# Block-sparse attention and a routed expert layer on one core: keys and values stacked on 128 partitions, first chunks in sequence order, two key sets and six V tiles

## The chip, the cores and the metric

The kernel runs on one core of one Trainium2 chip. TensorE (PE) multiplies 128x128 tiles from SBUF into PSUM; its weight loads are shown as an engine of their own (PEld). VectorE (DVE), ScalarE (ACT) and GpSimd (POOL) do the element-wise work, and SyncE (SP) issues most transfers. Each engine has its own in-order queue; semaphores link them. The metric is the device time of one execution in microseconds; lower is better.

## The reference

Two blocks run one after the other, all in float32. The first is attention with a block mask: 4 sequences, 8 heads, 768 positions, 64 dimensions a head, blocks of 32 positions (24 blocks). A query block sees its own block and its two neighbours, the first and the last block, and three blocks drawn at random for it; the first and the last query block see all blocks.

```python
mask = np.abs(blk_i - blk_j) <= window
mask = mask | (blk_i == 0) | (blk_j == 0) | (blk_i == n_blocks - 1) | (blk_j == n_blocks - 1)
for qb in range(n_blocks):
    for kb in sampled_blocks[qb]:
        mask[qb*block:(qb+1)*block, kb*block:(kb+1)*block] = True
attn = softmax(where(mask, q @ k.T / sqrt(D), -1e9));  out = attn @ v
```

The second takes the 3072 rows of 512 that result. Each row goes to one of 8 experts, the one whose embedding has the largest cosine with the row, and comes back as `gate * (relu(x @ w1[e]) @ w2[e])`, where w1 is 512x1024 and w2 is 1024x512 per expert.

## The kernel before

Attention runs in 24 steps over chunks of 128 query rows. Sequences go in pairs (0 and 1, then 2 and 3): `place(n)` maps chunk n to a pair, a chunk position c (0 to 5) and a member i of the pair, and chunks alternate between the members. Rows are shifted by 32, so that chunk c = 0 holds the last and the first block (the "end" rows, which see all keys) and two ordinary blocks; every other chunk has two halves of 64 rows. A pair of adjacent chunks shares one transfer of Q (`load_q`), one V tile (`load_v`, `vt`) and one gather of the random blocks' V (`gather_v`, `vg_ring`, two buffers).

For one chunk the work on PE is this.

- `turn_q` transposes Q into `qt`, which is block-diagonal over the two heads of a head pair: rows 0 to 63 are nonzero for head 0 only, rows 64 to 127 for head 1 only.
- `score_near` scores the queries against their own 64-key window and against the 64 end keys (`ke`, the last and the first block). It uses quarters of the array (64 rows x 64 columns), one head at a time; `near_at` says where each result goes.
- `score_far` scores the queries, per block of 32, against a gathered set of 128 keys: three random blocks and the outer neighbour block. Both heads go in one product.
- `weigh_near` and `weigh_far` multiply the exponentials with V into `av`. `vg0` is a copy of the end blocks' V (`keep_ends`), and `near_v` copies the neighbour block's V into `vg`.
- For c = 0, `score_ends` and `weigh_ends` do the end rows against all 768 keys.
- `normalize` divides by the sum of the weights; `turn_x` and `chunk_logits` (one step later) make the router's logits; `route` does the rest of the routing and ends with the transfer of the rows to `x_dram`.

`turn_x` and `turn_q` share one PSUM buffer, `xg_ps`. Scores and K transposes share a ring of two PSUM buffers, `big`.

Keys are transposed per head pair by `turn_k` from `kraw` (loaded by `load_k`; g counts 4 sequences x 4 head pairs). There are three key sets `kt` (sequence 3 uses that of sequence 0 again), and seven V tiles. `gather_k` copies the key blocks that a chunk needs into `kg`: one random block on DVE, two on POOL, the neighbours on DVE.

The order of the work in attention is written out by hand, in `attention_fast` (L1242): per step s, scores of chunk s, weighing of chunk s - 1, logits of chunk s - 2, with K transposes (`turning`), K loads (`loading`), V loads, Q loads and gathers placed by step number. SP issues in that order and waits at the first transfer whose buffer is not free. `after_step` (L1223) places the routing, the early dispatch and the loads of the first expert tile's weights at given steps. Before step 0, the kernel loads Q of both sequences, K of both, and all of the first pair's V.

After attention, 5 expert tiles of rows from the first pair and 20 tiles of the rest follow, each with 4 MB of weights in a ring of three (`fetch_weights`, L1091). The pool `wp` opens at step 18, in memory that the attention's short-lived buffers leave; `wp2` opens after attention.

Of the kernel before, what the change touches and what calls it, by code (L numbers as in the profile page):

```python
# [55 lines left out]
NV = NC + 1  # L56
# [334 lines left out]
def kset(b):  # L391

    return b if b < B - 1 else 0


def vtile(k, a, m):

    return k.vt[m if a == 0 else (NC + m) % NV]


def both(src, a):

    return src[DUO * a:DUO * (a + 1)].rearrange("i h s d -> s (i h) d")


def load_q(k, s):

    a, c = divmod(s, NC)
    k.raw["q", s] = t = k.ld.tile([P, DUO * H, D], F32, name="qraw", tag="qraw", bufs=2)
    src = both(k.q, a)  # L410
    return [(t[rows], src[lo:lo + rows.stop - rows.start]) for rows, lo in pieces(c)]


def load_k(k, g, pool=None):

    b, j = divmod(g, NPAIR)
    k.raw["k", g] = t = (pool or k.kld).tile([P, NC, 2, D], F32, name="kraw", tag="kraw", bufs=5 if pool else 3)
    return [(t[:, :, h], k.k[b, 2 * j + h].rearrange("(c p) d -> p c d", p=P)) for h in range(2)]


def load_v(k, a, m):

    v = vtile(k, a, m).rearrange("p i h e -> p (i h) e")
    src = both(k.v, a)
    return [(v[rows, :, 0:D], src[lo:lo + rows.stop - rows.start]) for rows, lo in pieces(m)]


def keep_ends(k, a, half):

    k.nc.gpsimd.tensor_copy(out=k.vg0[a][D * half:D * (half + 1)], in_=vtile(k, a, 0)[0:D])  # L430
# [14 lines left out]
def gather_v(k, s):  # L445

    a, c = divmod(s, NC)
    k.vg[s] = t = k.vg_ring[s % len(k.vg_ring)]
    src = both(k.v, a)
    for r in range(NRAND):  # L450
        for g, shift in zip(blocks_of(c), shifts(k, mybir.EngineType.SP, r, c)):
            yield (t[r * BLK:(r + 1) * BLK, g].rearrange("p i h e -> p (i h) e")[:, :, 0:D], src[bass.ds(shift, BLK)])


def fetch_all(k, n, loads):

    for i, (to, src) in enumerate(gather_v(k, n) if n is not None else ()):
# [8 lines left out]
def near_v(k, s, some):  # L466

    a, c = divmod(s, NC)
    for g in blocks_of(c):
        block = NG * c + g - 2 if g % 2 == 0 else NG * c + g  # L470
        if g in some and 0 < block < NB - 1:
            rows, m = home(block)
            k.nc.gpsimd.tensor_copy(out=k.vg_ring[s % len(k.vg_ring)][NRAND * BLK:P, g], in_=vtile(k, a, m)[rows])  # L473


def turn_k(k, g):
# [3 lines left out]
    kt, ke = k.kt[kset(b)], k.ke[kset(b)]  # L480
# [5 lines left out]
    copy(out=kt[:, j].rearrange("p (w t) -> p w t", w=2), in_=ps[:, :, 0:3 * P])  # L486
    if j == NPAIR - 1:
        for i, block in enumerate((NB - 1, 0)):
            nc.scalar.copy(out=ke[:, :, i * BLK:(i + 1) * BLK], in_=kt[:, :, block * BLK:(block + 1) * BLK])


def turn_q(k, n):

    i = n % DUO
    raw = k.raw["q", n // DUO]
    ps = ring(k, "xg_ps", 0, 1, k.eps, [P, ND, P])
    for j in range(NPAIR):
        lo = i * H + 2 * j
        k.nc.tensor.transpose(ps[:, j], raw[:, lo:lo + 2, :].rearrange("p h d -> p (h d)"), k.ident)  # L499
    k.qt[n] = t = k.qt_ring[n % 2]  # L500
# [5 lines left out]
def gather_k(k, n):  # L506
# [3 lines left out]
    kt = k.kt[kset(b)]  # L510
# [12 lines left out]
def near_at(j, half):  # L523

    odd = j % 2
    base = 2 * P * (j // 2)
    if half is None:
        return 1 - odd, base + D * odd
    return half, base + ((3 * D if odd else 2 * D) if half else (3 * D if odd else 0))


def score_near(k, n):
# [3 lines left out]
    kt, qt = k.kt[kset(b)], k.qt[n]  # L536
    ps = k.big.tile([P, 2, 512], F32, name="ac", tag="big")
    halves = (1,) if c == 0 else (0, 1)
    for j in range(NPAIR):
        for half in (None, *halves):  # L540
            r, lo = near_at(j, half)
            for h in range(2):
                rows = slice(D * h, D * (h + 1))
                if half is None:
                    cols = slice(D * halves[0], P)
                    keys = k.ke[kset(b)][rows, j]
                else:
                    cols = slice(D * half, D * (half + 1))
                    at = D * (2 * c + half) - BLK
                    keys = kt[rows, j, at:at + D]  # L550
                nc.tensor.matmul(ps[D * r:D * (r + 1), h, lo:lo + cols.stop - cols.start], lhsT=keys,  # L551
                                 rhs=qt[rows, j, h, cols], start=True, stop=True)
    k.pac[n] = e = k.pp.tile([P, 2, 512], F32, name="pac", tag="pac")
    if c:
        nc.scalar.activation(e, ps, ACT.Exp, scale=SCALE)
    else:
        for rows, cols in ((slice(D, P), slice(2 * D, 4 * D)), (slice(D, P), slice(0, D)), (slice(0, D), slice(D, 2 * D))):
            part = [x[rows].rearrange("p y (q w) -> p (y q) w", w=2 * P)[:, :, cols] for x in (e, ps)]
            nc.scalar.activation(part[0], part[1], ACT.Exp, scale=SCALE)
# [23 lines left out]
def score_ends(k, n, j):  # L583
# [3 lines left out]
    kt, ke, qt = k.kt[kset(b)], k.ke[kset(b)], k.qt[n]  # L587
    ps = k.big.tile([P, 2, 512], F32, name="bps", tag="big")
    for m in range(NC):
        for r in range(2):  # L590
            for h in range(2):
                rows = slice(D * h, D * (h + 1))
                lo = D * (2 * m + r) - BLK
                keys = ke[rows, j] if m == 0 and r == 0 else kt[rows, j, lo:lo + D]
                nc.tensor.matmul(ps[D * r:D * (r + 1), h, D * m:D * (m + 1)], lhsT=keys, rhs=qt[rows, j, h, 0:D],  # L595
                                 start=True, stop=True)
    k.pb[j] = e = k.pb_ring[j // 2]
    nc.scalar.activation(e.rearrange("p h m t -> p h (m t)"), ps[:, :, 0:NC * D], ACT.Exp, scale=SCALE)


def weigh_ends(k, n, pairs):

    b, c, i = place(n)
    for m in range(NC):
        for odd in range(2):
            for j in pairs:
                h = 2 * j + odd
                to = side(c, h, 0)
                weigh(k, n, slice(D * to, D * (to + 1)), h, k.pb[j][:, odd, m], vtile(k, b // DUO, m)[:, i, h])
# [18 lines left out]
def weigh_near(k, n, turn):  # L628

    b, c, i = place(n)  # L630
    if turn == 0:
        k.av[n] = two_banks(k, "av"), set()
    a = b // DUO
    e, v, v0 = k.pac[n], vtile(k, a, c), k.vg0[a]
    halves = (1,) if c == 0 else (0, 1)
    todo = ([], [])
    for j in range(NPAIR):
        for h in range(2):
            for own in (None, *halves):
                r, lo = near_at(j, own)  # L640
                if (r == j // 2) != (turn == 0):
                    continue
                rows = slice(D * r, D * (r + 1))
                for half in halves if own is None else (own,):
                    at = lo + D * (half - halves[0]) if own is None else lo
                    rhs = (v0 if own is None else v)[rows, i, 2 * j + h]
                    todo[r].append((side(c, 2 * j + h, half), 2 * j + h, e[rows, h, at:at + D], rhs))
    order = []
    for r in range(2):
        left = [[x for x in todo[r] if x[0] == to] for to in range(2)]  # L650
        order.append([x for pair in zip_longest(*left) for x in pair if x])
    for pair in zip_longest(*order):
        for x in pair:
            if x:
                to, h, lhsT, rhs = x
                weigh(k, n, slice(D * to, D * (to + 1)), h, lhsT, rhs, turn == 1)
# [4 lines left out]
def weigh_far(k, n):  # L661

    b, c, i = place(n)
# [940 lines left out]
```

## Time and profile before

| | us |
|---|---|
| median of 3 runs | 676.78 (674.54 to 678.27) |
| profiled execution, its own time | 673.24 |
| its span | 671.5 |
| PE matmuls busy, of the span | 606.3 (90%), 9016 records |
| DVE / ACT / POOL busy | 230.7 / 119.6 / 239.1 |
| HBM read and written | 156.65 MB and 12.90 MB |
| mean granted TensorE clock | 0.96 |

Busy PE is not PE at its peak: matmuls are pipelined, and records overlap. A float32 product shows as two matmul records. In a line of the chain of waits, the numbers are the start and the length in us; in the table of stretches, each engine's busy time is followed by its number of instructions. "SPq" is SP's queue, "issue" is time in which an engine waited for nothing that the profile shows. In a line of waits, the numbers are the total in us, the number of waits and the longest.

### The profile page before, as it was taken

Reading aid. Unit: us, or ns where it says so; the run is one execution under the profiler, and the core shown is the slowest. Engines: PE = TensorE matmul, PEld = TensorE weight load, DVE = VectorE, ACT = ScalarE, POOL = GpSimd, SP = SyncE. Lnnn points to the kernel's source line nnn. Section 1 sums busy time; section 2 is a strip of 40 time slices with the busy share of each in tenths; the row PEclk is TensorE's granted clock in tenths of the full one; section 3 lists DMA queues with packets and bytes.
Section 4 is the critical chain, followed back from the end, with each engine's and each line's share of the span. In section 5 each row is a group of like instructions: output and inputs, shape, how many; then the busy total and the mean of one; then the engine's idle time right before and its main releaser. Section 6 shows DMA issues by size and latency. Waiting matters only on the chain.

```text
span 671.5 us, 21249 instructions
## 1 busy us (share of the span) xinstructions
PE 606.3 (90%) x9016; PEld 472.5 (70%) x9016; DVE 230.7 (34%) x739; ACT 119.6 (18%) x267; POOL 239.1 (36%) x450
## 2 busy tenths in 40 slices
PE   4468989986888988799999999999999999999995
PEld 2457978876887887787777776675576665766773
DVE  2252444652533777542761112121121111121210
ACT  1233333442442433320000000000000001000000
POOL 1172234641532545431113443334333343433333
PEclk8788979997998998989999999999999999999999
DMA  9998589999858678958999999999899998999711
GB/s 162 191 205 119 111 138 177 172 186 189 152 87 112 119 139 137 242 196 282 403 398 411 376 345 345 347 326 323 312 412 392 406 381 308 404 399 394 296 48 32
DMA packets 187164, 170.77 MB, mean 254 GB/s; under 512 B 147560, under 2 KB 147688, under 8 KB 184242
## 3 DMA queue, kind: packets, MB, share of 16 engines
q1 hardware_dynamic: 177698, 154.82, 82.2%
q0 software_dynamic: 5216, 13.43, 5.7%
q10 hardware_dynamic: 4144, 1.05, 1.1%
q8 instruction: 73, 1.20, 0.8%
q14 instruction: 33, 0.27, 0.1%
HBM read 156.65 MB, written 12.90 MB: 252 GB/s over the span
## 4 chain that ended last, share of the span: by engine, by line
PE 81%; SPq 6%; issue 5%; DMA 3%; DVE 2%; ACT 1%; POOL 1%; POOLq 0%; DVEq 0%; ACTq 0%
PE hp L1154 25%; PE yp L1167 24%; PE av L619 11%; PE dps L573 4%; SPq L463 4%; PE yp L722 3%; PE ac L551 3%; PE hp L1199 2%; PE yp L1219 2%; PE bps L595 2%; PE xg_ps L499 2%; SPq L461 2%; DMA vt<-in_v_dram 2%; PE xg_ps L711 2%; DMA vg<-in_v_dram 1%
## 5 line engine op out<-in xcount | busy, mean ns | idle before, releaser
L1154 PEld LDWEIGHTS hp<-xgt,w 128*128 128x128 f32 x1472 | 167.8, 192 | 10.3 <-issue 10.2
L1154 PE MATMUL hp<-xgt,w 128*128 128x128 f32 x1472 | 169.3, 275 | 0.0
L1167 PE MATMUL yp<-w,h 128*128 128x512 f32 x368 | 161.9, 592 | 0.0
L1167 PEld LDWEIGHTS yp<-w,h 128*128 128x128 f32 x368 | 68.1, 190 | 76.5 <-issue 76.3
L1078 POOL DMA_INDIRECT xg<-x_dram,quarter x88 | 89.3, 1015 | 32.3 <-issue 27.4
L1180 POOL DMA_INDIRECT out_dram<-y,slot_l x20 | 20.5, 1025 | 155.9 <-DVE y L1179 155.9
L1157 ACT ACTIVATE h<-hp 128x512 f32<-128x512 f32 x23 | 13.7, 598 | 284.9 <-PE hp L1154 283.2
L473 POOL COPY vg<-vt 32x1040 f32<-32x1040 f32 x40 | 42.1, 1053 | 59.7 <-PE av L619 53.2
L516 POOL COPY kg<-kt 128x128 f32 x176 | 43.7, 295 | 46.9 <-issue 27.5
L1161 DVE TENSOR_SCALAR h<-hp 128x512 f32<-128x512 f32 x23 | 15.9, 691 | 127.8 <-PE hp L1154 127.8
L503 DVE COPY qt<-xg_ps 64x512 f32<-64x512 f32 x48 | 33.1, 689 | 64.3 <-PE xg_ps L499 63.5
L1179 DVE TENSOR_SCALAR y<-yp,gate 128x512 f32<-128x512 f32 x20 | 15.0, 750 | 102.2 <-PE yp L1167 90.1
L573 PE MATMUL dps<-qt,kg 128*64 128x64 f32 x1408 | 47.7, 224 | 2.0 <-issue 1.2
L619 PE MATMUL av<-vt,pac 64*64 64x65 f32 x704 | 46.5, 226 | 0.9 <-DVE x L811 0.7
L573 PEld LDWEIGHTS dps<-qt,kg 128*64 128x64 f32 x1408 | 43.9, 138 | 4.3 <-issue 1.4
L619 PE MATMUL av<-vg,pac 64*64 64x65 f32 x704 | 38.3, 234 | 4.1 <-issue 4.1
L619 PEld LDWEIGHTS av<-vt,pac 64*64 64x64 f32 x704 | 38.4, 140 | 3.1 <-issue 1.4
L619 PE MATMUL av<-vg,pd 128*32 128x65 f32 x1408 | 30.0, 233 | 7.4 <-issue 5.9
L578 ACT ACTIVATE pd<-dps,bias 128x256 f32<-128x256 f32 x88 | 34.7, 475 | 9.9 <-PE dps L573 9.8
L619 PEld LDWEIGHTS av<-vg,pac 64*64 64x64 f32 x704 | 30.2, 138 | 5.3 <-issue 4.7
L619 PEld LDWEIGHTS av<-vg,pd 128*32 128x32 f32 x1408 | 24.4, 116 | 12.9 <-issue 12.1
L551 PE MATMUL ac<-qt,ke 64*64 64x128 f32 (+1 forms) x384 | 29.2, 282 | 3.6 <-DVE qt L503 2.1
(229 smaller groups left out, 647.3 us busy)
## 6 DMA issues: line engine op xcount, KB each, us to landing
w<-in_moe_w_dram SPq DMA_DIRECT2D x52, 2048.0 KB, 13.6
vg<-in_v_dram SPq DMA_DIRECT2D x132, 128.0 KB, 5.2
kraw<-in_k_dram SPq DMA_DIRECT2D x32, 192.0 KB, 4.7
x_dram<-x SPq DMA_DIRECT2D x10, 516.0 KB, 4.5
vt<-in_v_dram SPq DMA_DIRECT2D x10, 512.0 KB, 6.7
qraw<-in_q_dram SPq DMA_DIRECT2D x9, 512.0 KB, 5.1
w<-in_moe_w_dram SPq DMA_DIRECT2D x8, 512.0 KB, 8.1
xg<-x_dram,quarter POOLq DMA_INDIRECT x88, 6.2
```

The source lines that it names most:

```text
L463: k.nc.sync.dma_start(out=to, in_=src)
L473: k.nc.gpsimd.tensor_copy(out=k.vg_ring[s % len(k.vg_ring)][NRAND * BLK:P, g], in_=vtile(k, a, m)[rows])
L503: k.nc.vector.tensor_copy(out=t[rows, :, h], in_=ps[rows])
L516: copy(out=t[:, :, g, s * BLK:(s + 1) * BLK], in_=kt[:, :, bass.ds(shift, BLK)])
L551: nc.tensor.matmul(ps[D * r:D * (r + 1), h, lo:lo + cols.stop - cols.start], lhsT=keys, rhs=qt[rows, j, h, cols], start=True, stop=True)
L573: nc.tensor.matmul(out[D * r:D * (r + 1), NG * j + g], lhsT=kg[:, j, g, D * r:D * (r + 1)], rhs=qt[:, j, :, cols], start=True, stop=True)
L578: nc.scalar.activation(e[:, :, g].rearrange("p j h t -> p j (h t)"), out.rearrange("p (j g) h t -> p j g (h t)", g=NG)[:, :, g], ACT.Exp, ...
L619: k.nc.tensor.matmul(av[lanes, h // NPAIR, h % NPAIR * P:h % NPAIR * P + D + 1], lhsT=lhsT, rhs=rhs, start=first[0], stop=last, skip_group ...
L1078: k.nc.gpsimd.indirect_dma_start(out=x[:, g], out_offset=None, in_=quarters, in_offset=bass.IndirectOffsetOnAxis(ap=k.quarter[:, g, t:t + ...
L1154: nc.tensor.matmul(hp[:, f, :], lhsT=w1[:, d, (f0 + f) * P:(f0 + f + 1) * P], rhs=xt[:, d, :], start=(d == 0), stop=(d == ND - 1))
L1167: nc.tensor.matmul(yp, lhsT=h[:, f, :], rhs=w2[:, f, :], start=(f == 0), stop=(f == NF - 1))
L1180: k.scattered = nc.gpsimd.indirect_dma_start(out=k.out[:, :], out_offset=bass.IndirectOffsetOnAxis(ap=slot, axis=0), in_=y[:, :], in_offse ...
```

## The change

It has these parts.

1. **Near products.** The end keys move to the last 64 columns of `kt`. `score_near` scores own keys for both heads of a pair in one product over 128 rows (own keys to output partitions 0 to 63, end keys to 64 to 127). `st_ring`, two buffers per member pair, holds on its upper 64 partitions the chunk's own V (`stack`, on ACT) and on its lower 64 the end blocks' V (`stack_ends`, on POOL), so `weigh_near` does own and end keys in one product of 128 rows. `near_at`, `keep_ends` and `vg0` go.
2. **End rows.** For head pairs 0 and 1, `score_ends` takes 128 keys and both heads in one product; pairs 2 and 3 stay as they were.
3. **Order.** `TURNS` runs the chunks as 0, 2, 1, 3, 4, 5, ...: the first two chunks of sequence 0, then the first two of sequence 1. Q, V and the gathers of the first pair are loaded by sequence (argument i), sequence 0 first; five K loads stand before step 0 instead of eight.
4. **Buffers.** Two key sets instead of three, six V tiles instead of seven, five `kraw` buffers. K transposes of sequences 2 and 3 move to steps 10 to 12, their loads to steps 4 to 11, V loads of the second pair to steps 4 to 10.
5. **Within a step.** `weigh_far` is in two parts, with `turn_q` between them (except where end rows are done). Where K is turned, `gather_k` follows the turning.
6. **Tail.** `wp` holds only the first w1; the first w2 goes to `wp2`, and its transfers are issued after attention, as are the last two `x_dram` transfers of attention's routing.

```diff
+TURNS = [0, 2, 1, 3, *range(4, NCH)]
...
+def stack(k, s, i=None):
+    st, c = k.st_ring[s % 2], s % NC
+    for half in (1,) if c == 0 else (0, 1):
+        k.nc.scalar.copy(out=st[0:D, half, which(i)], in_=k.vt[c][D * half:D * (half + 1), which(i)])
+def stack_ends(k, s, halves, i=None):
+    for half in halves:
+        k.nc.gpsimd.tensor_copy(out=k.st_ring[s % 2][D:P, half, which(i)], in_=k.vt[0][0:D, which(i)])
...
 def score_near(k, n):
+        for half in halves:
+            at = D * (2 * c + half) - BLK
+            nc.tensor.matmul(out[0:D, j, half], lhsT=kt[:, j, at:at + D], rhs=qt[:, j, :, D * half:D * (half + 1)],
+                             start=True, stop=True)
+            if half == halves[0]:
+                nc.tensor.matmul(out[D:P, j, half:2].rearrange("p f h t -> p h f t"), lhsT=kt[:, j, S:S + D],
+                                 rhs=qt[:, j, :, D * half:P].rearrange("p h (f t) -> p h f t", t=D), start=True,
+                                 stop=True)
...
 def score_ends(k, n, j):
+    if j < NPAIR // 2:
+        for m in range(NC):
+            lo = m % 3 * P
+            out = ps[:, m // 3, lo:lo + P].rearrange("p (h t) -> p h t", h=2)
+            for rows, at in [(slice(0, P), P * m - BLK)] if m else [(slice(0, D), S), (slice(D, P), BLK)]:
+                nc.tensor.matmul(out[rows], lhsT=kt[:, j, at:at + rows.stop - rows.start], rhs=qt[:, j, :, 0:D],
+                                 start=True, stop=True)
...
 def weigh_near(k, n, turn):
+    for hh in range(2 * turn, 2 * turn + 2):
+        for h in (hh, hh + NPAIR):
+            for half in (1,) if c == 0 else (0, 1):
+                to = side(c, h, half)
+                weigh(k, n, slice(D * to, D * (to + 1)), h, e[:, h // 2, half, D * (h % 2):D * (h % 2 + 1)],
+                      st[:, half, i, h], turn == 1)
...
 def fetch_weights(k, i, at, pieces=1):
+        w = ring(k, name, load, 3, k.wp if load % 3 < 1 and name == "w1" else k.wp2, shape)
...
 def after_step(n, b):
-        step = partial(next, fetch_weights(n, 0, 0, 4), None)
-        plan += [(s + i // 3, 1, step) for i in range(9)]
+        n.first_weights = fetch_weights(n, 0, 0, 4)
+        plan += [(s + i, 1, partial(next, n.first_weights)) for i in range(4)]
...
 def attention_fast(n, ctx):
-    for g in range(2 * NPAIR):
-        fetch_all(n, None, load_k(n, g, n.setup if g < 5 else None))
-    fetch_all(n, None, load_v(n, 0, 0))
+    for g in range(5):
+        fetch_all(n, (), load_k(n, g))
+    for m in range(2):
+        fetch_all(n, (), load_v(n, 0, m, 0))
...
+    fetch_all(n, gather_v(n, 0, 0), [])
+    for m in range(2, NC):
+        fetch_all(n, (), load_v(n, 0, m, 0))
     turn_q(n, 0)
     for g in range(NPAIR):
         turn_k(n, g)
+        if g + 5 < 2 * NPAIR:
+            fetch_all(n, (), load_k(n, g + 5))
+    fetch_all(n, gather_v(n, 1, 0), load_q(n, 0, 1))
+    for m in range(NC):
+        fetch_all(n, (), load_v(n, 0, m, 1))
+    fetch_all(n, gather_v(n, 0, 1), load_q(n, 1, 1))
+    fetch_all(n, gather_v(n, 1, 1), [])
...
-    turning = {0: range(NPAIR, 2 * NPAIR), 3: (8,), 5: (9,), 7: (10,), 9: (11,), 10: (12, 13), 11: (14, 15)}
-    loading = {1: (8,), 3: (9,), 5: (10,), 7: (11, 12), 9: (13, 14), 10: (15,)}
+    turning = {10: (8, 9), 11: (10, 11, 12), 12: (13, 14, 15)}
+    keys_at = {4: (8,), 5: (9,), 6: (10,), 7: (11,), 8: (12,), 10: (13, 14), 11: (15,)}
+    values_at = {4: (0,), 5: (1,), 6: (2,), 8: (3,), 9: (4,), 10: (5,)}
...
+        for part in range(2):
+            if last is not None:
+                weigh_far(n, last, part)
+            if after is not None and part == 0 and not ends:
+                turn_q(n, after)
...
         if s == 1:
+            for g in range(NPAIR, 2 * NPAIR):
+                turn_k(n, g)
+            keys_gathered()
...
 def fast(n):
+        for _ in n.first_weights:
+            pass
+        for steps in n.unwritten:
+            for _ in steps:
+                pass
```

## The prediction

> **What bounds the kernel now.** I read the stretches first. I cut the span at the starts of step 0 (21.2 us), step 2 (60.7), step 4 (83.2), step 13 (178.0) and the first expert tile (305.5). Each row gives length, busy time of PE, PEld, DVE, ACT and POOL, granted clock, DMA share and GB/s.
>
> ```profile
> 0.00:21.20 21.20, 11.02 (x38) 6.52 (x39) 7.09 (x23) 3.58 (x6) 3.64 (x20) 0.84 1.07 175
> 21.20:60.70 39.50, 23.60 (x512) 20.92 (x513) 12.69 (x44) 10.10 (x20) 17.50 (x42) 0.79 1.24 186
> 60.70:83.20 22.50, 22.01 (x743) 20.70 (x744) 10.53 (x33) 9.55 (x20) 6.83 (x19) 1.00 0.48 91
> 83.20:178.00 94.80, 80.89 (x2304) 74.24 (x2301) 47.72 (x170) 34.69 (x84) 37.51 (x100) 0.93 0.98 168
> 178.00:305.50 127.50, 110.01 (x3389) 100.64 (x3385) 67.70 (x257) 44.35 (x105) 54.61 (x144) 0.96 0.79 148
> 305.50:671.50 366.00, 358.74 (x2049) 249.49 (x2048) 84.94 (x216) 17.33 (x32) 118.99 (x127) 1.00 0.89 336
> ```
>
> The experts (366.0 us) are PE from end to end and the change does not touch their matmuls. The opening has PE busy 60% of the time under full queues. The middle (steps 4 to 12) has the queues full, 0.98. The late stretch has PE bound with queue room. The chain of waits, in order of time, says what the opening waits for:
>
> ```profile
> 20.79 0.80 SPq L463
> 21.63 1.03 SPq L463
> 22.70 6.73 DMA vt<-in_v_dram
> 29.45 0.34 SPq L461
> 29.84 6.42 DMA vt<-in_v_dram
> ```
>
> SP sends sixteen K transfers and then V; POOL's copies and everything behind them wait for V of both sequences. The waits of PE in the middle (first fence) and in the late stretch (second):
>
> ```profile
> PE kps L484 <- DMA kraw<-in_k_dram: 5.6, 1, 5.6
> PE av L619 <- issue: 4.5, 5, 2.6
> ```
>
> ```profile
> PE av L619 <- issue: 5.5, 5, 2.8
> PE bps L595 <- issue: 3.2, 3, 1.2
> PE xg_ps L499 <- DVE xt L713: 2.1, 1, 2.1
> PE xg_ps L711 <- issue: 2.0, 2, 1.0
> ...
> PE ac L551 <- issue: 1.0, 2, 0.5
> ```
>
> "Issue" is 11.7 us of the late stretch. I read it as instruction supply, because the page has
>
> ```profile
> PE 606.3 (90%) x9016; PEld 472.5 (70%) x9016; DVE 230.7 (34%) x739; ACT 119.6 (18%) x267; POOL 239.1 (36%) x450
> ...
> q8 instruction: 73, 1.20, 0.8%
> ```
>
> 1.20 MB in 73 packets is 16.4 KB each, and 18,032 PE instructions over 73 are 247 a packet; PE's issue gaps in the trace lie at multiples of about 256 PE instructions.
>
> **What the skill says.** "Runtime: NRT & Kernel Launch", Instruction fetch mechanics: an engine's instructions come in 16 KiB blocks of 256, and the fetch is mostly hidden. The block size agrees; hidden it is not (issue gaps up to 2.8 us). "TensorE: Matmul & The Clock Gate", Part 3: products on different row or column groups of the array run together. The trace agrees: far scores (L573), 128 rows by 64 columns on alternate halves, pass 64 matmuls of 64 columns in 2.02 us (31.6 ns each), while full-array matmuls of 128 columns (L1154) take 7.14 us for 64 (111.6 ns). "DMA: Bandwidth & Descriptors", Specifications: transfers under 512 B miss line rate; Q, K and V move here in 256-byte pieces, at 168 to 186 GB/s against 336 in the experts.
>
> **The change part by part.** A float32 product is two matmul records.
>
> Near scores, per ordinary chunk (c above 0, 20 of 24): 48 records become 24. Before, four quarters of the array ran together: about 1.1 us from the first record to the far scores. After, the contraction covers two heads, half of it zeros in qt: 16 records of 128 columns on one half beside 8 of 256 on the other. Two L1154-sized matmuls side by side cost 55.8 ns each, so 4096 columns / 128 x 55.8 = 1.8 us: **+0.7**, x20 = +14. For c = 0, 16 records x 55.8 = 0.9, as before.
>
> Near weighing: 64 records, in the chain as two rows of 0.86 us, become 32 of the form that the end rows use (pb: 48 records from 201.80 to 203.35, 32.3 ns): 1.03, **-0.69**, x20 = -14. For c = 0, two times 0.86 become 16 x 32.3 = 0.5: -1.2, x4 = -5.
>
> End-row scores of pairs 0 and 1: 48 records, 0.86 us (199.38 to 200.24), become 14: 10 x 111.6 + 4 x 55.8 = 1.34, **+0.48**, x8 = +4.
>
> TensorE's own work therefore stays as it is: +14 - 14 - 5 + 4 = -1. What falls is the count: 544 + 704 + 272 = 1520 matmuls and as many weight loads, 22% of attention's (9016 - 2049 = 6967). An ordinary step goes from 256 matmuls to 200, 400 instructions, 1.6 blocks instead of 2.
>
> Stack copies: two of 64 x 1040 on ACT every other step. No row has them on ACT; its 128 x 1024 exponential takes 1010 ns (L555), so 1.0 us each, and not below the 0.80 of its 768-wide kt copy. ACT is busy 44 of 127 us late; they stand behind the step's exponentials and ahead of sq. Without that cover they cost PE 2 us every other step, 10 late. stack_ends replaces keep_ends on POOL (1.05 us each, about +5 in all); POOL is at 43% late. Nothing for either.
>
> turn_q now stands after half of weigh_far, on the one xg_ps buffer that turn_x fills. DVE's xt copy ends 0.73 us after turn_x's last matmul; half of weigh_far is 1.04 / 2 = 0.52. PE waits 0.2 to 0.3 us a step, 8 late steps: +2 (0 if it falls into a block gap; +4 with DVE late). Behind it stand the rest of weigh_far and the logits. The two copies to qt still have 0.5 + 0.8 + 0.5 us of PE work ahead of the next scores.
>
> Opening. Sequence 0 comes first: half Q (0.5 MB), K 0 to 4 (1.9), V 0 and 1 (0.5), six gathers (0.4), V 2 to 5 (1.0): 4.3 MB / 186 GB/s + 2 = 25 us, where the last V of before was issued at 40.7. The transfers are halves, so SP issues more of them (each at least 0.35 us, 0.8 when the queue is full: the queue, not SP, sets the pace). Step 0 starts at about 19, step 1 at 25 (POOL's stack, near V and eight kg copies stand ahead). Step 1 is near 1.8, far 2.0, end scores 2 x 1.34 + 2 x 0.87, weighing 0.5 + 0.5 + 2 x 1.55, turn_q 0.6, four turn_k 2.6: 15.5 us, at a clock of 0.85 18: to 43. Two more for the kt copy and sequence 1's gather. Step 2, 6 us and a wait for Q: 53. Step 3, 14.4: 68 to 69. Before, step 4 started at 83.2: **-14** (-5 to -18).
>
> Middle. The K and V loads of before's steps 1 and 3 (1.8 MB) wait until steps 4 and later, and two key sets push all eight turn_k into steps 10 to 12. From step 4 to the last K pair: V 3.1, K 3.1, Q 2.1, gathers 2.7, x_dram 4.1 = 15.1 MB; before moved 13.3 MB from 81 to 156, 177 GB/s. SP restarts about 5 us into step 4 (Q and gather wait for turn_q and weigh_far): 5 + 85 = 90 us, and 6 more for turn_k 15 and the rest of step 12: 96 against 94.8, **+1**. PE's own floor is 9 x 8.2 + 5 + 4 = 83 (-12); at 145 GB/s it is 115 (+20).
>
> Late. Of 11.7 us of issue three quarters go: -9. The clock of 0.96 costs at most 5; cold phases follow gaps: -2.5. turn_q +2; matmuls 0. **-9** (-2 to -15).
>
> Experts. Tile 0's w2 moves from a pool opened at step 18 to one whose memory I expect free at step 22 (kt's last reader), still ahead of its use in the second half of tile 0: 0 (to +5: 2 MB at 400 GB/s). Two x_dram writes go behind it; the first rows of late tiles that need them are far off.
>
> Sum: 673.24 (span 671.5 and 1.7 around it) - 14 + 1 - 9 = 651 for the profiled execution. The median of before lies 3.5 above its profiled execution; I add 3: **654**.
>
> **The rivals.**
> 1. *The middle takes back the opening.* The moved 1.8 MB cost 1.8 / 168 = 11 us that nothing hides. For: DMA 0.98 there. Against: the queues at 0.48 in steps 2 and 3. 665 (660 to 672).
> 2. *The queues keep up* and PE's floor holds in the middle: 654 - 12 = 642. For: slices above 200 GB/s. Against: the 5.6 us wait for K.
> 3. *No change*: gaps and stalls only move. 677.
> 4. *Slower:* the column halves do not overlap when one has 128 columns and the other 256. Then near scores take 16 x 111.6 + 8 x 215 (half of L1167's 429) = 3.5 us, 1.7 more in 20 steps: 688. It decides from 2.9 us a chunk, where the 22 us are gone. Against: far scores overlap, with equal lengths.
>
> **How the numbers follow.** Forecast 0.50 (645 to 662); rival 1 0.20; rival 2 0.12; rival 3 0.07; rival 4 0.11. Half a per cent is what this measurement can tell: faster 0.82, within 0.07, slower 0.11. Down to 640 for most of rival 2, up to 673 for rival 1: about 0.8.
>
> **What would show it.** Right: step 4 near 69 us, step 13 near 165; 56 fewer matmuls and under 0.3 us of issue in an ordinary step; near scores 1.8 us, near weighing 1.0; a short wait of turn_q for xt in most steps; waits for kraw at steps 10 to 12; experts at 366. Wrong: step 4 after 78 us, a middle above 110, near scores near 3.5, or a wait of the first yp for w2.

## The result, and the profile after

| | before | after |
|---|---|---|
| median, same chip | 675.66 us (674.39 to 678.27) | 669.05 us (667.05 to 670.61) |
| ratio after / before | | 0.990 (0.985 to 0.994) |
| profiled execution, its own time (span) | 673.24 (671.5) | 670.42 (668.7) |

The change makes the kernel 1.0% faster. The forecast was 654 us. The sign is right, but 669 us lies outside the 645 to 662 given for the forecast itself and only inside the wide range of 640 to 673: 6.6 us of some 23 came.

The stretches of the profile after are cut at the same events as those of before: the starts of step 0, step 2, step 4, step 13 and the first expert tile. The columns are the same (length; busy time of PE, PEld, DVE, ACT and POOL; granted clock; DMA share; GB/s).

```profile
0.00:16.80 16.80, 11.23 (x38) 6.75 (x38) 5.33 (x11) 2.28 (x3) 3.05 (x17) 1.00 0.94 170
16.80:46.50 29.70, 22.16 (x441) 19.23 (x440) 15.06 (x59) 13.63 (x26) 11.72 (x35) 0.94 0.83 160
46.50:74.40 27.90, 24.43 (x536) 22.61 (x537) 8.64 (x26) 9.85 (x19) 15.73 (x37) 0.88 0.86 154
74.40:179.80 105.40, 83.51 (x1818) 75.11 (x1816) 51.48 (x172) 42.53 (x91) 38.85 (x103) 0.88 0.97 166
179.80:302.75 122.95, 115.98 (x2632) 105.96 (x2629) 67.82 (x256) 55.16 (x114) 54.63 (x143) 0.91 0.74 130
302.75:668.70 365.95, 358.73 (x2052) 250.55 (x2048) 85.18 (x216) 17.30 (x32) 119.79 (x128) 1.00 0.90 342
```

Step 4 starts at 74.4 us instead of 83.2: the opening gained 8.8. The middle (steps 4 to 12) went from 94.8 us to 105.4: it lost 10.6, more than the opening gained. The late stretch gained 4.5, the experts nothing. -8.8 + 10.6 - 4.5 is -2.7, the difference of the two spans but for rounding. So the question is why the middle grew, and why the late stretch gave so little.

The waits of PE, in the middle and then in the late stretch (total in us, number, longest):

```profile
PE av L622 <- DVE x L799: 15.0, 1, 15.0
PE kps L493 <- DMA kraw<-in_k_dram: 5.2, 3, 2.5
PE xg_ps L506 <- DVE xt L701: 1.0, 5, 0.2
```

```profile
PE xg_ps L506 <- DVE xt L701: 5.4, 8, 1.9
PE av L622 <- issue: 0.8, 2, 0.4
PE av L622 <- DVE x L799: 0.7, 1, 0.7
```

"Issue" fell from 11.7 us to 0.8 in the late stretch and is gone from the list of the middle (7.4 us before): that part of the change works. In its place stand two waits: one of 15.0 us in step 8, and turn_q's wait for `xt`. The name on the 15.0 us, L799, is not the cause. It is a small routing instruction of DVE, and the chain of waits, in order of time, says what held DVE:

```profile
113.87 2.91 SPq L470
...
120.31 0.68 SPq L808
...
121.04 4.34 DMA x_dram<-x
...
125.50 0.10 DVE x L686
...
126.11 0.21 DVE x L799
126.33 1.14 PE av L622 x16
```

Read from the end: PE waits for DVE; DVE stands at L686 (`normalize`), which writes a new `x`; the `x` tiles are a ring of three, one for each pair of chunks, and the fourth pair (chunk 6) takes the buffer of the first, whose rows have to be in `x_dram` first. That transfer (L808) stood behind step 6's gathers and loads (L470) in SP's queue. In the kernel before it was issued at 110.6, ahead of the chunk-6 `normalize` at 124.9, and nothing waited. Since the new order brings the first pair's second chunk to step 2 instead of 1, its routing and its transfer come one step later, at step 7, behind all the loads of step 6.

The page of after, its count of TensorE instructions and of instruction blocks:

```profile
PE 616.0 (92%) x7496; PEld 480.2 (72%) x7496; DVE 233.5 (35%) x739; ACT 140.8 (21%) x285; POOL 243.8 (36%) x461
...
q8 instruction: 61, 1.00, 0.7%
```

9016 - 7496 = 1520 matmuls fewer, as counted, and 61 blocks instead of 73. An ordinary step of after (step 6; start, length, then what):

```profile
90.98 0.27 PE L542 MATMUL ac<-qt,kt 128*64 128x128 f32 x1
...
92.72 2.04 PE L567 MATMUL dps<-qt,kg 128*64 128x64 f32 x64
94.58 0.64 PE L622 MATMUL av<-st,pac 128*64 128x65 f32 x16
95.16 0.66 PE L699 MATMUL xg_ps<-ident,x 128*128 128x128 f32 x4
95.74 0.66 PE L622 MATMUL av<-vg,pd 128*32 128x65 f32 x32
96.60 0.66 PE L506 MATMUL xg_ps<-ident,qraw 128*128 128x128 f32 x4 [0.19 <-DVE xt L701]
...
98.76 0.69 PE L622 MATMUL av<-st,pac 128*64 128x65 f32 x16
99.28 0.27 PE L542 MATMUL ac<-qt,kt 128*64 128x128 f32 x1
```

Near scores take 92.72 - 90.98 = 1.74 us (forecast 1.8): the 128-column products on one half of the array do run beside the 256-column ones on the other. Near weighing takes 0.58 + 0.52 = 1.10 (forecast 1.03). turn_q waits 0.19. The step takes 8.30 us.

### The profile page after: what moved, and what is told of

It reads as the page before. It is cut to its first block, busy times and chain, and to the rows that moved or that the text cites. A ratio compares the mean times of both kernels' runs of the same rounds, so it can differ in the third digit from the quotient of the medians.

```text
span 668.7 us, 18349 instructions
## 1 busy us (share of the span) xinstructions
PE 616.0 (92%) x7496; PEld 480.2 (72%) x7496; DVE 233.5 (35%) x739; ACT 140.8 (21%) x285; POOL 243.8 (36%) x461
## 4 chain that ended last, share of the span: by engine, by line
PE 82%; DVE 5%; SPq 5%; DMA 4%; issue 2%; ACT 1%; POOL 0%; DVEq 0%; POOLq 0%
PE hp L1142 25%; PE yp L1155 24%; PE av L622 8%; PE dps L567 5%; PE yp L710 4%; PE ac L542 3%; DMA kraw<-in_k_dram 3%; PE ac L545 2%; SPq L470 2%; PE xg_ps L506 2%; PE hp L1187 2%; PE yp L1207 2%; SPq L472 2%; PE xg_ps L699 2%; DVE xt L701 1%
## 5 line engine op out<-in xcount | busy, mean ns | idle before, releaser
L1149 DVE TENSOR_SCALAR h<-hp 128x512 f32<-128x512 f32 x23 | 15.9, 691 | 146.4 <-PE hp L1142 140.0
L482 POOL COPY vg<-vt 32x1040 f32<-32x1040 f32 (+1 forms) x45 | 43.2, 960 | 62.4 <-PE av L622 60.3
L542 PE MATMUL ac<-qt,kt 128*64 128x128 f32 x352 | 48.7, 296 | 2.1 <-DVE qt L511 2.1
L567 PEld LDWEIGHTS dps<-qt,kg 128*64 128x64 f32 x1408 | 49.0, 143 | 1.6 <-POOL vg L482 1.5
L545 PE MATMUL ac<-qt,kt 128*64 128x256 f32 (+1 forms) x192 | 48.1, 399 | 0.8 <-ACT kt L498 0.8
L622 PE MATMUL av<-st,pac 128*64 128x65 f32 x704 | 33.0, 239 | 15.7 <-DVE x L799 15.7
L542 PEld LDWEIGHTS ac<-qt,kt 128*64 128x64 f32 x352 | 43.2, 152 | 3.1 <-ACT st L434 1.9
L622 PEld LDWEIGHTS av<-st,pac 128*64 128x64 f32 x704 | 27.5, 150 | 16.5 <-issue 16.0
L622 PE MATMUL av<-vg,pd 128*32 128x65 f32 x1408 | 31.9, 234 | 0.8 <-issue 0.8
```

The costliest lines, as they stand in the source:

```text
L482: k.nc.gpsimd.tensor_copy(out=k.vg_ring[s % 2][NRAND * BLK:P, g, which(i)], in_=k.vt[m][rows, which(i)])
L542: nc.tensor.matmul(out[0:D, j, half], lhsT=kt[:, j, at:at + D], rhs=qt[:, j, :, D * half:D * (half + 1)], start=True, stop=True)
L545: nc.tensor.matmul(out[D:P, j, half:2].rearrange("p f h t -> p h f t"), lhsT=kt[:, j, S:S + D], rhs=qt[:, j, :, D * half:P].rearrange("p h ...
L567: nc.tensor.matmul(out[D * r:D * (r + 1), NG * j + g], lhsT=kg[:, j, g, D * r:D * (r + 1)], rhs=qt[:, j, :, cols], start=True, stop=True)
L622: k.nc.tensor.matmul(av[lanes, h // NPAIR, h % NPAIR * P:h % NPAIR * P + D + 1], lhsT=lhsT, rhs=rhs, start=first[0], stop=last, skip_group ...
```

## The experiments

Four theories. **A**: the late transfer of the first pair's rows (the 15 us) took the gain. **B**: SP's queues bound the middle, and the stall stands only where other waits for K, V and Q would stand. **C**: the fetch of TensorE's instructions is what the near products relieve. **E**: turn_q between the halves of `weigh_far` costs more than was counted. Ratios are to the kernel before on the same chip, in three groups of four kernels (671.26, 669.43 and 670.10 us before); they come from the single executions and can differ by some 0.002 from the quotient of the medians. Between groups, ratios are compared and not times.

| | run | median, us | ratio (95%) |
|---|---|---|---|
| e1 | after, early transfer | 663.03 | 0.988 (0.983 to 0.994) |
| e2 | before, near products alone | 652.49 | 0.970 (0.963 to 0.976) |
| e3 | after, turn_q behind weigh_far | 658.89 | 0.981 (0.975 to 0.987) |
| e4 | before, late transfer | 671.99 | 1.000 (0.998 to 1.003) |
| e5 | e1 and e3 together | 653.88 | 0.977 (0.974 to 0.980) |
| e6 | e5, K of sequence 2 in steps 2 and 3 | 654.86 | 0.976 (0.974 to 0.979) |
| e7 | e5, end rows as before | 658.21 | 0.981 (0.979 to 0.984) |
| e8 | e2, K 13 a step earlier | 648.28 | 0.968 (0.965 to 0.971) |
| e9 | e5, gathers of pair 1 whole | 657.98 | 0.983 (0.980 to 0.987) |
| e10 | e9 and e6 together | 650.82 | 0.972 (0.967 to 0.976) |
| e11 | e3 with the old order | 675.55 | 1.010 (1.006 to 1.015) |
| e12 | e8, end rows as changed | 651.07 | 0.972 (0.968 to 0.975) |

The profiled executions of e1, e9 and e10 lie 5 to 7 us under their medians, so their stretches flatter them; the ratios decide.

### e1 and e4: the transfer moved

e1 puts the first pair's transfer back to step 6, part 0, ahead of that step's loads; e4 moves it to step 7 in the kernel before.

```diff
 # e1, in after_step of the changed kernel
-    plan += [(s + 1 + i // 2, i % 2, routing) for i in range(4)]
+    plan += [(s + 1 + i // 2, i % 2, routing) for i in range(4)] if b else [(s + 1, i // 2, routing) for i in range(4)]
     if s + 3 < NCH:
-        plan += [(s + 3, 0, routing)]
+        plan += [(s + 3 if b else s + 2, 0, routing)]
 # e4, in after_step of the kernel before
-    plan += [(s + 1 + i // 2, i % 2, routing) for i in range(5)]
+    plan += [(s + 1 + i // 2 + (b == 0 and i == 4), i % 2, routing) for i in range(5)]
```

Expected of e1:

> The changed kernel, with the routing of pair 0 drawn together so that its transfer to x_dram stands at step 6 ahead of step 6's loads, where the kernel before had it, instead of at step 7 behind them. Theory A (the wait of 15 us in step 8 is the place of this one transfer on SP's queue: the third x buffer is not free for the normalisation of chunk 6 until it has landed): step 8 falls from 24.8 us to about 8.3, the cold clock after it goes too, and the time falls by 14 to 18, from 669 to 651 to 655. Rival B (the queues are simply full in the middle, and a wait removed here comes back as a wait for K): the waits for kraw in steps 10 to 12 grow from 5 us to 15 or more, and the time stays at 664 to 669.

Expected of e4:

> The kernel before with only the transfer of pair 0 to x_dram moved from step 6 to step 7, where the changed kernel has it. Theory A: normalisation of chunk 6 waits for it here too, step 7 or 8 grows by 4 to 14 us, and the time is 680 to 690. Rival: SP reaches it soon enough in this kernel, since step 6 asks for less here (1.3 MB against 2.2), and the time stays at 674 to 678.

In e1 step 8 falls from 24.8 to 8.3 us: the mechanism of A is shown. The time hardly moves: steps 5, 6, 9 and 12 are longer by 1.7, 1.2, 6.9 and 1.6 us. The waits of PE in steps 3 to 13 of e1:

```profile
PE kps L493 <- DMA kraw<-in_k_dram: 8.3, 3, 3.6
PE xg_ps L506 <- DVE xt L701: 2.3, 5, 1.5
```

Here K is waited for 8.3 us instead of 5.2, less than the 15 that B expected. By the ratios (0.988 beside 0.990) the edit alone gives nothing that can be told from zero. e4, the same cause put into the kernel before, made step 8 3.9 us longer and the whole no longer. A stall of 15 us that costs at most a few is what B says: the queue was behind anyway.

### e2: the near products alone

The kernel before with part 1 of the change and nothing else of it, with one `st` buffer in the place of `vg0` (and, to make room, one `xt` buffer and two scratch tiles in `pb_ring`). The end keys stay in `ke`.

```diff
+        for half in halves:
+            at = D * (2 * c + half) - BLK
+            nc.tensor.matmul(out[0:D, j, half], lhsT=kt[:, j, at:at + D], rhs=qt[:, j, :, D * half:D * (half + 1)],
+                             start=True, stop=True)
...
+            if s % 2 == 0 and s // DUO < NS:
+                if s // DUO == NC:
+                    stack_ends(n, NC, (1, 0))
+                stack(n, s // DUO)
```

> The kernel before with part 1 of the change alone (near scores of two heads in one product, own and end V stacked on 128 partitions, one stack buffer filled at the end of the step that frees it); order, end rows, key sets and V tiles as before. Three small buffers are shared to make room. Theory C (the issue waits are the supply of PE's instructions, and fewer instructions remove them although TensorE's own work stays the same): issue on PE between steps 4 and the experts falls from 20 us to under 5, ordinary steps from about 9.4 to 8.3 to 8.7, and the time from 676 to 660 to 668. Rival D (issue has another cause, such as transfers that are late): the waits stay, steps stay at 9 or more, and the time is 674 to 678.

3.0% faster, three times the gain of the whole change and more than was expected. The stretches of steps 4 to 12 and 13 to the end of attention:

```profile
79.75:168.24 88.49, 78.07 (x1805) 73.27 (x1805) 47.20 (x170) 42.73 (x91) 36.17 (x98) 0.92 1.04 178
168.24:289.11 120.87, 110.36 (x2764) 103.60 (x2765) 67.90 (x256) 55.60 (x114) 56.41 (x146) 0.92 0.83 155
```

The middle is 6.3 us shorter than before, the late stretch 6.6, the opening 3.4, while PE's busy time over the span is 603.6 us against 606.3, at a mean clock of 0.949 against 0.962. What fell are the waits for issue. Of the 11.7 us in the late stretch these are left:

```profile
PE bps L587 <- issue: 2.3, 1, 2.3
PE av L611 <- issue: 1.3, 1, 1.3
```

From step 0 to the end of attention they fall from 21.5 us to 7.6, 14 of the 16.4 us by which the profiled span is shorter. Those that are left, and all of before's, lie a multiple of 256 TensorE instructions apart in the trace, within two (counted for waits above 0.3 us). C holds: the gain comes from 1248 matmuls and as many weight loads fewer (7768 records), hardly from TensorE's arithmetic. "Runtime: NRT & Kernel Launch", Instruction fetch mechanics, calls the fetch mostly hidden; in an ordinary step of before, with 512 TensorE instructions, it was not; with 400 in 8.1 to 8.7 us it nearly is. It follows that the other parts of the change together cost 2% (0.990 beside 0.970).

### e3 and e5: where turn_q stands

e3 puts turn_q behind both parts of `weigh_far`; e5 has this and the early transfer.

```diff
-            if after is not None and part == 0 and not ends:
+            if after is not None and part == 1 and not ends:
                 turn_q(n, after)
```

> The changed kernel with turn_q behind the whole of weigh_far again. Theory E (the move brought the waits of turn_q for the xt copy, 6.4 us, and in steps 18 and 19 the cold clock behind them): those waits fall under 1 us, and the time falls by 4 to 9, to 660 to 665. Rival F (the move was needed, because the shorter near weighing no longer covers the two copies to qt): the near scores of each ordinary step wait 0.4 us or more for qt, 16 times, and the time is 669 to 676.

> The changed kernel with both single edits: the first x_dram transfer at step 6 ahead of that step's loads, and turn_q behind the whole of weigh_far. Theory A+E (two separate losses, the late transfer and the wait for xt, which add): step 8 falls from 28 to about 9 us with all else as in the run with the whole weigh_far, so 645 to 650 us, a ratio to the kernel before near 0.963; step 4 to step 13 about 95 us. Rival B (the queue is the bound of the middle, and the stall only stood where waits for K, V and Q would have stood): steps 9 to 12 grow by 8 to 15 us instead, step 4 to step 13 stays above 101 us, 654 to 660 us, ratio 0.972 to 0.982.

e3 has 0.981 beside 0.990, e5 0.977 beside e1's 0.988: the place of turn_q costs about 1%, some 6 to 8 us, twice over. In e3's late stretch the wait falls, and ordinary steps take 8.0 to 8.1 us instead of 8.3:

```profile
PE xg_ps L506 <- DVE xt L701: 2.2, 3, 1.0
PE ac L542 <- DVE qt L511: 0.8, 5, 0.2
```

So 3.2 us of waits and about 0.2 us in each of some sixteen ordinary steps: 6 us. E holds, though the waits stay above the 1 us that it expected. The whole late stretch of e3 is

```profile
178.87:290.74 111.87, 107.78 (x2629) 99.90 (x2629) 68.45 (x256) 55.41 (x114) 55.33 (x145) 0.97 0.84 147
```

11.1 us shorter than in after, with 8.2 less of PE's busy time, at a clock of 0.97 instead of 0.91. Not all of that is turn_q's place: in e1, with turn_q where the change has it and 4.6 us of waits, the clock is 0.97 as well and the stretch 115.8. In e5 the stall is gone and the late stretch is shorter than was forecast, but the middle is not (rows of the middle and of the late stretch):

```profile
70.45:173.67 103.22, 87.30 (x1817) 79.89 (x1813) 51.75 (x173) 43.22 (x91) 38.70 (x101) 0.88 1.18 171
173.67:284.26 110.59, 104.63 (x2629) 96.88 (x2629) 68.10 (x256) 55.36 (x114) 54.94 (x144) 1.00 0.84 148
```

103.2 us with step 8 at 10.4 instead of 28.2 (e3): the rival B, as its expectation had it (step 9 went to 13.8 us, step 12 to 19.9). Its waits of PE in the middle begin with

```profile
PE kps L493 <- DMA kraw<-in_k_dram: 8.6, 3, 3.6
PE av L622 <- DMA vg<-in_v_dram: 3.3, 5, 0.9
```

The queue is full and moves 103.22 x 171 = 17.7 MB in the stretch; before, it moved 94.8 x 168 = 15.9.

### e6, e9 and e10: why steps 2 and 3 carry so little

In the opening the DMA share of after is 0.83 to 0.86 (1.24 before), at 154 to 160 GB/s. SP's own queue in e5, around steps 2 and 3 (start, length until the next thing, transfers):

```profile
49.67 12.36 SPq L470 DMA_DIRECT2D vg<-in_v_dram  x18
62.12 0.29 SPq L1301 DMA_DIRECT2D x_dram<-zero  x1
62.50 0.41 SPq L472 DMA_DIRECT2D qraw<-in_q_dram  x1
...
64.49 10.47 SPq L470 DMA_DIRECT2D vg<-in_v_dram  x10
```

The 18 half gathers of one sequence are 65.5 KB each and take 12.36 / 18 = 0.69 us each to issue: 95 GB/s. So SP's issuing, not the transfers, is the limit there. e6 moves the K loads of sequence 2 to steps 2 and 3, and the first of sequence 3 (g = 12) from step 8 to step 4, which its expectation calls unchanged; e9 gathers pair 1 in 12 whole transfers instead of 24 halves; e10 does both.

```diff
 # e6, e10
-    keys_at = {4: (8,), 5: (9,), 6: (10,), 7: (11,), 8: (12,), 10: (13, 14), 11: (15,)}
+    keys_at = {2: (8, 9), 3: (10, 11), 4: (12,), 10: (13, 14), 11: (15,)}
 # e9, e10
-    fetch_all(n, gather_v(n, 1, 0), load_q(n, 0, 1))
+    fetch_all(n, gather_v(n, 1), load_q(n, 0, 1))
...
-    fetch_all(n, gather_v(n, 1, 1), [])
```

> As the run with both edits, and the K loads of sequence 2 (g 8 to 11) in steps 2 and 3, where SP's queue was waiting, instead of steps 4 to 7; g 12 stays about where it was (step 4). Theory B' (the middle is bound by the 1.6 MB that the change put there, the queue has room in steps 2 and 3): the waits of the K transposes for kraw at steps 10 to 12 (8.3 us with the early transfer alone) fall below 3 us, step 4 to step 13 is at most 95 us, and the time is 6 to 10 us below that of the run with both edits. Rival: steps 2 and 3 are lengthened by what the middle gains (Q and the gathers of steps 4 and 5 come later), time within 3 us of the run with both edits.

> As the run with both edits (ratio 0.977), and the gathers of chunk pair 1 as 12 whole transfers instead of 12 for sequence 0 and 12 for sequence 1. Theory G (SP's issuing is the limit in the opening: the 36 half gathers take about 0.7 us each to issue, 65 KB each, 95 GB/s, while the whole ones of later steps reach 140): SP reaches the loads of step 2 some 8 us earlier than at 62.5 us. Alone it gives little, since what comes next in the queue waits for the V buffer that step 3 frees: within 3 us of the run with both edits, but steps 4 and 5 no longer wait for Q. Rival: the 0.8 MB ahead of sequence 1's V delays steps 2 and 3: 2 to 5 us slower.

> The run before with the K loads of sequence 2 in steps 2 and 3 too. Theory G: the time that SP no longer spends on half gathers now carries the 1.6 MB of K, so that step 4 to step 13 falls from 103 to about 95 us: 6 to 8 us below the run with both edits, ratio 0.965 to 0.968. Rival (the transfers themselves, not their issue, are the limit all the way to step 12): within 2 us of the run with both edits, ratio 0.974 to 0.979.

e6 is e5's equal, as its rival had it. The K loads are not issued before 62 us either, and push back Q and the gathers of the next steps (step 5 takes 14.5 us instead of 8.7). e9 alone is slower than e5 by 0.6%, as its rival had it; its profile does not show why. Together they give 0.972 beside e5's 0.977, between the theory's range and the rival's, a difference about as large as its uncertainty. But e10 and e9 differ in the place of the K loads alone and ran in one group: 650.82 us beside 657.98, with intervals that lie apart. The stretches of steps 2 and 3 and of the middle in e10:

```profile
47.29:74.51 27.22, 24.31 (x535) 22.66 (x534) 8.65 (x26) 9.85 (x19) 15.70 (x37) 0.87 1.01 184
74.51:166.05 91.54, 79.98 (x1816) 73.43 (x1813) 51.81 (x173) 43.23 (x91) 38.31 (x101) 0.94 1.04 173
```

Steps 2 and 3 carry 184 GB/s, where e5 has 144 and e9 152. They last 27.2 us as in e9 (22.8 in e5), and the middle falls to 91.5 us, from 98.7 in e9 and 103.2 in e5: step 13 starts at 166.1 us instead of 173.3 and 173.7. Seven of the sixteen K transfers of the middle are issued before it in e10, and it moves 91.54 x 173 = 15.8 MB instead of e9's 16.7. So bytes were a good part of what made the middle long. That the half gathers kept them out of steps 2 and 3 is seen in the profiles of e6 and e10 (a middle of 102.4 and 91.5 us); the ratios of these two, 0.976 and 0.972, do not separate it.

### e11: the old order with the new buffers

e3 with `TURNS` in plain order, Q, V and gathers of both sequences in one transfer, and what hangs on it (stack, K transposes of sequence 1, the first pair's transfer) where the kernel before has it.

```diff
-TURNS = [0, 2, 1, 3, *range(4, NCH)]
+TURNS = list(range(NCH))
...
-        fetch_all(n, (), load_v(n, 0, m, 0))
+        fetch_all(n, (), load_v(n, 0, m))
...
-        if s in (2, 3):
-            loads += load_q(n, s)
+        if s in (0, 2):
+            loads += load_q(n, 2 + s // DUO)
```

> The changed kernel with turn_q behind the whole of weigh_far, and the order of the kernel before put back (chunks 0, 1, 2, 3; Q, V and gathers of both sequences in one transfer; stack, K transposes of sequence 1 and the first x_dram transfer where the kernel before has them); near products, end rows, two key sets, six V tiles and the tail stay as changed. Theory H (the order costs: it takes 9 us out of the opening and loses more in the middle through half transfers): step 4 near 80 us, step 13 at 165 to 170, 644 to 650 us, ratio 0.962 to 0.971, under the run with both edits. Rival I (the two key sets cost, which put the transposes and loads of sequence 2 into the middle): step 4 near 80 us, step 13 at 178 or later, ratio 0.982 to 0.990, over the run with both edits.

Slower than before, and outside both ranges of the expectation; less the 15.4 us explained below it lies where rival I had it. The first fence is PE's wait for K between 17 and 75 us, the second the middle.

```profile
PE kps L493 <- DMA kraw<-in_k_dram: 17.0, 3, 15.4
```

```profile
92.87:193.32 100.45, 85.17 (x1811) 77.98 (x1811) 49.55 (x171) 42.86 (x91) 37.83 (x100) 0.88 1.02 166
```

15.4 us are of this run's own making: with five `kraw` buffers the last K loads of sequence 1 come behind all of V, and the old order needs them in step 0. The middle is free of that, and at 100.5 us it is as long as with the new order. So it isn't the order that lengthens the middle. With near products and end rows as changed, but the buffers as before, it takes 86.6 us (e12). What lies between is above all the fourth part of the change, two key sets and six V tiles with their loads and K transposes from step 4 on; the place of `gather_k` in the fifth part was not run apart from it. The order in turn is what the five `kraw` buffers need: it asks for the keys of sequence 1 one step later.

### e7, e8 and e12: end rows, and K 13

e7 is e5 with the end-row scores of all head pairs in the old form. e8 is e2 with one load moved. e12 is e8 with the new end-row scores for head pairs 0 and 1, as in the change.

```diff
 # e7, in score_ends
-    if j < NPAIR // 2:
+    if j < 0:
 # e8, e12
-    loading = {1: (8,), 3: (9,), 5: (10,), 7: (11, 12), 9: (13, 14), 10: (15,)}
+    loading = {1: (8,), 3: (9,), 5: (10,), 7: (11, 12), 8: (13,), 9: (14,), 10: (15,)}
 # e12, in score_ends
+    if j < NPAIR // 2:
+        for m in range(NC):
...
+            for rows in (slice(0, P),) if m else (slice(0, D), slice(D, P)):
+                keys = kt[:, j, P * m - BLK:P * m - BLK + P] if m else kt[:, j, BLK:BLK + D] if rows.start else ke[:, j]
+                nc.tensor.matmul(out[rows], lhsT=keys, rhs=qt[:, j, :, 0:D], start=True, stop=True)
```

> As the run with both edits, with the end-row scores of head pairs 0 and 1 in the form of the kernel before (48 matmul records on quarters of the array instead of 14 on 128 keys and both heads). Theory by TensorE's columns: each of the eight chunks with end rows gets 0.48 us shorter, the time is 4 us below that of the run with both edits. Rival, instruction supply: 272 matmuls and as many weight loads more in all, in steps that have over 500 TensorE instructions already, cost what the columns give: within 2 us of it, or slower, with waits of kind issue in the steps with end rows.

> The kernel before with the near products alone (ratio 0.970), and the load of K 13 at step 8 instead of 9 (one place earlier; K 14 stays at 9). If the 8.0 us wait of step 10 for kraw is a matter of order within the queue: the wait falls to 3 us or less, ratio 0.960 to 0.965. If the queue is simply full: another wait (gathered V or Q of steps 9 to 11) takes its place, ratio 0.968 to 0.972.

> The kernel before with the near products, K 13 one step earlier (ratio 0.968), and the changed form of the end-row scores for head pairs 0 and 1. If what the end rows gave in the changed kernel (0.0042 of the time, through fewer TensorE instructions) holds here too: ratio 0.963 to 0.966, the fastest of all. Rival: here the steps with end rows wait for other things: 0.967 to 0.970.

The old form in e7 is 4 us slower, not faster, as its rival had it, and the waits for issue come back. From its late stretch, the first two lines, and e5's, the third:

```profile
PE av L622 <- issue: 2.8, 4, 1.0
PE bps L598 <- issue: 2.4, 1, 2.4
PE av L622 <- issue: 0.3, 1, 0.3
```

That is C seen from the other side, with instructions added. In e12 the new form gives nothing, rather 2 us the other way (0.972 beside 0.968). The two differences are about as large as their uncertainty and of opposite sign: what the end rows are worth stays open, within 4 us. In e8 the 8.0 us wait for K of step 10 becomes two, of 4.2 and 4.1 us, and the ratio is 0.968 beside e2's 0.970, which the intervals don't separate: its second branch. e2, e8, e10 and e12 all beat both kernels (the changed one at a ratio of 0.990); e8, at 648.28 us, has the lowest median and the lowest ratio.

## Why the prediction was right and wrong

**Right.** Near scores 1.8 (1.74 measured), near weighing 1.03 (1.10), 1520 matmuls fewer, ordinary steps almost without waits for instructions, the experts at 366. The rival in which the column halves do not overlap is out.

**Opening, -14: the measured -8.8 lies in its bounds.** Step 0 starts at 16.8 and step 2 at 46.5, near what was worked out (19 and 45). The rest is steps 2 and 3: 27.9 us where 6 + 14.4 and a wait were reckoned, at a clock of 0.88, with 3.3 us for Q. In e1, e3, e5, e6 and e7 step 4 starts at 70.5 to 72.2, with a clock of 0.93 to 1.00 in these two steps; in e9 and e10 at 74.6 and 74.5, with 0.87. So some 3 of the missing 5 us go with the clock of a single profile. "The queue, not SP, sets the pace" is wrong for half gathers, where SP does, but that this made the opening longer is not shown: e9 and e10, with two thirds of the half gathers made whole, reach step 4 no sooner.

**Middle, +1: measured +10.6. This is the step that broke the forecast, and the term that was mis-sized is its bytes.** "From step 4 to the last K pair" had 15.1 MB at 177 GB/s. What the profile after moved from the start of step 4 to the last K transposes (74.4 to 172.5 us):

```profile
DMA packets 59118, 16.88 MB, mean 172 GB/s; under 512 B 58094, under 2 KB 58094, under 8 KB 59100
...
vg<-in_v_dram SPq DMA_DIRECT2D x45, 128.0 KB
```

V, K and Q were counted right. The gathers, put at 2.7 MB, are 45 transfers of 131 KB, 5.9 MB; the `x_dram` transfers, put at 4.1, are 2.1. So 16.9 MB took 98 us where 90 were reckoned. The rate was a little high, too: the trace of before has 171 GB/s for the stretch from 81 to 156 us that the 177 was read from. The rest of step 12 took 7.3 us instead of 6. Over the whole middle 105.4 x 166 = 17.5 MB were moved, 1.6 more than before, at the same rate: 1.6 / 166 GB/s = 10 us. By the transfers issued, 1.4 of these are a V tile, two K transfers and four gathers. That is the first rival as it was written, with its mechanism (1.8 MB that nothing hides, 11 us) and its range, 660 to 672 us. The evidence against it, room in the queues of steps 2 and 3, was an argument about before; after, SP fills that room with issuing, and no load was placed there.

**A deadline that was not seen.** The prediction moved the routing a step later without listing what its last transfer releases: the `x` buffer of pair 0, due at the chunk-6 `normalize`. It shows as the 15.0 us of step 8, PE's largest wait in the profile. By e1 and by e5 beside e3 its removal is worth 0 to 3 us, as the queue's lateness then shows elsewhere.

**Late, -9: measured -4.5.** Issue gave 10.9 us, more than the 9 forecast. turn_q was put at +2 with "+4 with DVE late"; its waits are 5.4 us here, and e3 and e5 measure 6 to 8 over the whole run. The waits of 1.8 and 1.9 us in steps 18 and 19 come where DVE has the early dispatch ahead of the `xt` copy. The clock was to give 2.5 us and went from 0.96 to 0.91 instead, and PE's busy time from 110.0 to 116.0 us; how much of that belongs to the change is open, since e1 has 0.97 with turn_q in the same place.

**What the gain was and where it went.** Near products alone: -3.0%. The whole change: -1.0%. turn_q takes back 1% of the difference; the loads and K transposes that the fourth part puts into the full middle, and the half gathers, are most of the rest: e10, with some of these loads earlier and two thirds of the half gathers made whole, is again at e2's level. How the rest divides between loads, transposes and gathers is not settled.

## What to carry to other kernels

When a step is moved, follow its last instruction, too: which buffer does its transfer free, who takes that buffer next, and what stands ahead of it in the queue. When a stretch is bound by transfers, count the bytes from its first event to its last and compare with the same two events before; bytes pushed into a full stretch cost their time (here 1.6 MB at 166 GB/s, 10 us), and a big named stall in such a stretch may be worth almost nothing (here 15 us, 0 to 3). List the transfers behind a count of bytes one by one: here one entry was less than half of what the trace shows. Where TensorE waits for "issue" at regular counts of instructions, fewer and larger matmuls pay even if the columns stay the same.

## What was not expected of the hardware

TensorE ran at half clock for whole stretches. After turn_q's wait of 1.77 us in step 18 of after (first fence), the granted clock is 0.50 for 6.8 us (second fence, the stretches up to that point, of half clock, and behind it):

```profile
242.28 0.75 PE L506 MATMUL xg_ps<-ident,qraw 128*128 128x128 f32 x4 [1.77 <-DVE xt L701]
```

```profile
236.00:242.70 6.70, 4.93 (x135) 4.53 (x130) 5.64 (x33) 3.20 (x7) 0.00 (x0) 1.00 0.62 121
242.70:249.50 6.80, 6.80 (x80) 6.34 (x79) 3.66 (x13) 0.99 (x4) 4.38 (x12) 0.50 0.97 153
249.50:256.40 6.90, 4.99 (x152) 4.42 (x154) 6.12 (x18) 4.59 (x7) 6.45 (x16) 0.99 1.39 153
```

In that stretch TensorE does 80 matmuls in 6.8 us of unbroken work. In the trace such stretches, each a multiple of 3.4 us long, make 47.8 us of the steps from 4 on in the profile after, and 23.9 in that of before. A wait of 2.3 us for the same `xt` in e5's late stretch was followed by none, its clock there being 1.00, so a wait of this length does not suffice; what else it takes is open.
